# Re-laying copies behind units' products, and weight sums in earlier stretches, in a fused attention and feed-forward kernel

## The chip, the cores and the metric

The kernel runs on one core of a Trainium2 chip. The metric is the device time of one execution in microseconds. A core has a matrix engine (TensorE, PE in the profile), a vector engine (VectorE, DVE), an engine for activation functions (ScalarE, ACT), GpSimd (POOL), and a queue engine (SyncE, SP) that issues transfers. Each engine takes its instructions in the order in which they were written for it, and waits at an instruction until what it needs is there. Inputs and weights are in device memory; SBUF and PSUM are the core's own memories. [...]

## The reference

```python
B, H, S, D = 8, 12, 448, 64              # batches, heads, tokens, head size
scores = q @ k.transpose(0, 1, 3, 2) / sqrt(D) - log(S)
attn = 1 / (1 + exp(-scores))            # a sigmoid, no softmax
x = (attn @ v)                           # heads side by side: 3584 tokens x 768
gate = maximum(x @ w_gate, 0)            # 768 x 1536
val = x @ w_val                          # 768 x 1536
out = (gate * val) @ w_out               # 1536 x 768, float32
```

## The kernel before, in words

**Staging.** The kernel is software-pipelined over the eight batches: while TensorE does the attention of batch b it also does the feed-forward part of an earlier batch, in pieces put between pieces of attention. The order on every engine is written out by hand.

**Attention.** A batch has three groups of four heads (g) and seven chunks of 64 keys (c), so 21 score units. One unit (`qk_unit`, its products in line 239) makes scores into two PSUM banks, and ScalarE applies the sigmoid (line 187). When a group's seven chunks are there, `pv_group` multiplies with v (line 257) into two banks, and VectorE copies the result to the transposed activations xT (line 184).

**Feed-forward.** One unit (`gv`, lines 322 to 343) makes a gate and a value product (`g_ps`, `v_ps`, one bank each) for 128 of the 1536 inner columns; the gate goes through a relu on ScalarE (line 334) or VectorE (line 336), and VectorE multiplies it with the value into hT (line 343). When that product is done, the unit's value bank can be used again. Banks are given out in turn from a ring of eight (`bank`). A score unit, a PV group and a feed-forward unit each take two.

**Batch 1** has six stretches. Each is a burst of 3, 3, 3, 4, 4 or 4 score units, and then `ffn_mix` with 4, 3, 3, 3, 3 or 4 feed-forward units of batch 0. The bursts of the fourth and the sixth stretch hold a PV group after their second score unit. Batch 2's first burst (four score units with a PV group after the second) comes right behind the sixth stretch. In the code stretches and bursts count from 0: the fifth stretch is `hooks[4]` and `given[4]`.

**Hooks.** `ffn_mix` counts `left`, the units still to do, down from the number of units to 0. At each count it first runs the hooks whose number is at least `left`, then as many steps of the weight sums as `given` says for that place, then one unit. So `(3, ...)` in a stretch of three units runs ahead of the first, `(2, ...)` behind the first, and `(0, ...)` behind the last.

**Re-laying batch 2.** From batch 2 on, the heads' q and k are transposed by a DMA. `dma_transposes(b, g)` lets VectorE copy the group's k and then its q into one buffer `rel` (line 222, two copies), and has SP issue one transposing DMA from it to `qkT` (line 226). There are two `rel` buffers, so group 2's copies of a batch need group 0's transposing DMA to have read. The copies of batch 2 also need its k and q loads, which POOL issued earlier, and its first burst needs `qkT` of group 0.

**Late loads.** `late_loads` re-lays batch 2's third group, lets POOL copy two numbers out of `qkT` of the second group (`hold`, line 863, so that POOL goes on only when that transposing DMA has landed), and then lets POOL issue the loads of batch 2's v, of batch 3's k and q, and of `wo`, the output weights.

**Weight sums.** The feed-forward part of batch 1 saves products by using sums of weight blocks. For four pairs of 128 inner columns VectorE makes them beforehand in batch 1: `early_sum_steps` gives four steps for a pair, one in place on `wv` (`gate_sums`, line 391) and then S2, S1 and S4 (lines 391, 584, 391), 128 x 768 each. That is 16 steps in a fixed order; `given` says how many of them run at each place of a stretch. The step in place on `wv` must come behind batch 0's units on those columns.

Of the kernel before, what the change touches and what calls it, by code (L numbers as in the profile page):

```python
# [18 lines left out]
def kernel(  # L19
# [87 lines left out]
    def load(b, g0, g1, which, c0=0, c1=NCH):  # L107
        for nm, t16, src in zip("kq", tiles_of(b), (k, q)):
            if nm in which:
                xs, cs = slice(2 * g0, 2 * g1), slice(c0 * D, c1 * D)  # L110
                nc.gpsimd.dma_start(t16[:, xs, cs], rows_of(src, b)[:, xs, cs])  # L111

    def load_v(b):
        v16 = tiles_of(b)[2]
        nc.gpsimd.dma_start(v16[:, 0::2, :], rows_of(v, b)[:, 0::2, :])
        for r in range(2):
            nc.gpsimd.dma_start(
                v16[64 - 64 * r : P - 64 * r, 1::2, :], rows_of(v, b)[64 * r : 64 * r + 64, 1::2, :]
            )
# [70 lines left out]
    def qkT_of(b, g):  # L190
        if (b, g) not in qkT_tiles:
            qkT_tiles[(b, g)] = qkTp.tile([P, TW, P], FP16, tag="qkT", name="qkT")
        return qkT_tiles[(b, g)]
# [24 lines left out]
    def dma_transposes(b, g):  # L218
        k16, q16, _ = in_tiles[b]
        rel = relp.tile([P, TW, P], FP16, tag="rel", name="rel")  # L220
        for ti, t16 in enumerate((k16, q16)):
            nc.vector.tensor_copy(  # L222
                rel[:, ti * NCH : (ti + 1) * NCH, :].rearrange("p c (h d) -> p h c d", h=2),
                t16[:, 2 * g : 2 * g + 2, :].rearrange("p h (c d) -> p h c d", c=NCH),
            )
        nc.sync.dma_start_transpose(
            qkT_of(b, g)[:], rel[:].rearrange("p c x -> p (c x)")
        )
# [70 lines left out]
    def qk_unit(b, g, c):  # L299
        ps = [bank("qk_ps") for _ in range(2)]  # L300
        qk(qkT_tiles[(b, g)], c, 0, NCH, lambda hh: ps[hh][:, 0:S])
        PT = PTp.tile([P, 2, S], FP16, tag="PT", name="PT")
        for hh in range(2):
            sigmoid(PT[:, hh, 0:S], ps[hh][:, 0:S])
        PT_tiles[(b, g, c)] = PT

    def pv_group(b, g):
        pv(b, g, 0, S, [PT_tiles.pop((b, g, c))[:, :, 0:S] for c in range(NCH)])
# [74 lines left out]
    def open_late():  # L383
        first_sbuf.close()
        pool = ctx.enter_context(tc.tile_pool(name="late", bufs=1))
        late["T"] = pool.tile([P, 4, HF, HM], FP16, tag="T", name="T")
        late["X"] = pool.tile([P, 3, HD, S], FP16, tag="X", name="X")
        late["sums"] = ctx.enter_context(tc.tile_pool(name="sums", bufs=2))
# [174 lines left out]
    def early_sum_steps(j, f):  # L563
        views = []
        for i in range(3 * j, 3 * j + 3):
            t = early.tile([P, 2, 512], FP16, tag=f"PT{i}", name="S")
            flat = t[:].rearrange("p a y -> p (a y)")[:, 0 : HD * 2 * P]
            views.append(flat.rearrange("p (x y) -> p x y", y=2 * P))
        yield lambda: gate_sums(f, f + 2)
        yield from unit_sum_steps(("s", f), f, views)  # L570
# [285 lines left out]
    def pv_finish(b):  # L856
        pv_group(b, NG - 1)
# [7 lines left out]
    def both(b, g):  # L865
        pe_transposes(b, g, 0)
        pe_transposes(b, g, 1)
# [15 lines left out]
    def push_group(g):  # L883
        tail = [("y", g, p) for p in range(3)]
        if g == 0:
            work.extend([("u", 1, 8), ("s", 1, 0), ("u", 1, 9), ("s", 1, 4), ("u", 1, 10), ("u", 1, 11)])
            work.extend([tail[0], ("t", g, 0), ("t", g, 1), *tail[1:]])
            return
        if g != 2:
            tail.insert(0, ("y", g, NPP) if g == 3 else ("t", g, 2))  # L890
        work.extend([("w", g, f) for f in range(0, NFC, 2)] + tail)
# [40 lines left out]
    for b in range(1, B):  # L932
        if b == 1:
            cuts, pv_at = (0, 3, 6, 9, 13, 17, 21), {3: (0, 2), 5: (1, 2)}
        else:
            cuts, pv_at = (0, 4, 7, 11, 14, 18, 21), {0: (-1, 2), 2: (0, 2), 4: (1, 2)}
        bursts = list(range(len(cuts) - 1))
        inner = {}
        if b > 2:
            inner = {0: 1, 3: 5} if b == 3 else {0: 1} if b % 2 == 0 else {2: 3, 3: 5} if b == B - 1 else {4: 5}  # L940
            for n in inner.values():
                bursts.remove(n)
        count = len(bursts)
        hooks = {}
        if b == 1:
            mix = (4, 3, 3, 3, 3, 4)
            hooks = {
                1: [(3, lambda: both(1, 1))],
                3: [(3, lambda: both(1, 2))],
                4: [(3, lambda: dma_transposes(2, 0)), (1, lambda: dma_transposes(2, 1))],  # L950
                5: [(4, late_loads)],
            }
            steps = itertools.chain.from_iterable(early_sum_steps(j, 2 * j) for j in range(4))
            given = ((0, 0, 1, 1, 1), (0, 1, 1, 0), (0, 1, 1, 1), (0, 1, 1, 0), (2, 0, 0, 0), (0, 1, 1, 1, 1))
        else:
            mix = (0,) * count

        def burst(n):
            for i, (g, c) in enumerate(order[cuts[n] : cuts[n + 1]]):
                if n in pv_at and i == pv_at[n][1]:  # L960
                    if n == 0:
                        pv_finish(b - 1)
                        if b == 2:
                            push_group(0)
                        elif b % 2 == 0:
                            push_group(b // 2 - 1)
                    else:
                        pv_group(b, pv_at[n][0])
                qk_unit(b, g, c)

        for m in range(count):
            jobs, ahead = [], []
            burst(bursts[m])
            if m == 0 and b > 3:
                jobs.append(lambda: dma_transposes(b, 2))
            if b == 2 and m == 2:
                ahead.append(lambda: dma_transposes(3, 0))
            elif b == 2 and m == 3:
                jobs.append(lambda: dma_transposes(3, 1))
            elif b == 3 and m == count - 1:  # L980
                jobs.append(lambda: dma_transposes(4, 1))
            elif 0 <= m - count + 2 and 3 < b < B - 1:
                jobs.append(lambda: dma_transposes(b + 1, m - count + 2))
            if b == 1:
                if m == 0:
                    load(2, 0, 1, "kq")
                    load(2, 1, 2, "kq")
                    load(2, 2, 3, "kq")
            elif m == 0 and b + 1 < B:
                for g0, g1 in ((0, 1), (1, NG)) if b == 3 else ((0, NG),) if b > 3 else ():  # L990
                    jobs.append(lambda g0=g0, g1=g1: load(b + 1, g0, g1, "kq"))
                jobs.append(lambda: load_v(b + 1))
            if b == 2 and m == 0:
                ahead.append(lambda: split_sums(1))
            elif b == 2 and m == 4:
                open_late()
                first_sums = token_sum_steps(0, 0)
                ahead += [*first_sums[:2], lambda: weight_sums(0)]
            elif b == 2 and m == 5:
                ahead += [lambda: weight_sums(1), lambda: dma_transposes(3, 2)]  # L1000
                jobs += first_sums[2:]
            elif b == 3 and m == 0:
                jobs.append(lambda: (weight_sums(2), weight_sums(3)))
            elif b == 3 and m < 3:
                jobs.append(lambda: gate_sums(6 + 2 * m, 8 + 2 * m))
            if b % 2 and b > 2:
                if m == count - 1:
                    jobs.append(lambda: (batch_sums_t1(b // 2), batch_sums(b // 2, (0, 1))))
            elif b > 3 and m == 0:
                jobs.append(lambda: batch_sums(b // 2 - 1, (1, HD)))  # L1010
            if mix[m]:
                for job in jobs:
                    job()
                ffn_mix(mix[m], hooks.get(m, ()), steps, given[m])
            else:
                next_work(
                    jobs, ahead=ahead,
                    amid=(lambda: burst(inner[m])) if m in inner else None,
                )
            if b == 3 and m == count - 2:  # L1020
                dma_transposes(4, 0)
# [35 lines left out]
```

## Time and profile before

| what | value |
|---|---|
| three runs | 389.72 us median (389.47 to 389.98) |
| profiled execution, its own time | 390.76 us |
| its span, first to last instruction | 388.9 us |
| mean granted clock of TensorE | 0.998 |
| TensorE busy | 382.5 us, 98% of the span |
| VectorE busy | 300.1 us, 77% |
| ScalarE busy | 227.6 us, 59% |
| GpSimd busy | 49.9 us, 13% |
| instructions | 8973 |

A row of a timeline reads: start in us from the span's start, duration in us, engine, line of the kernel, operation, output<-input, shape, and in brackets the idle time of the engine before it and what ended it. Instructions of one kind that follow each other are merged (x12). Of the merged ones the duration reaches from the first start to the last end, and ends overlap the next start. A row of the chain that ended last reads: start, duration, what. A row of stretches of time reads: from:to, the time in it, then busy time and number of instructions of PE, PEld (weight load), DVE, ACT and POOL, then the granted clock, the mean busy share of the DMA engines, and GB/s.

### The profile page before, as it was taken

The numbers are of one execution on the slowest core, as the hardware profiler recorded it, in microseconds if no ns is written. First come the engines' busy times: TensorE is split into PE (matmuls) and PEld (weight loads), VectorE is DVE, ScalarE is ACT, GpSimd is POOL, SyncE is SP. The second block draws the span as 40 slices with busy tenths as digits, with TensorE's granted clock in tenths as the row PEclk, the third lists the DMA queues.
The fourth block names the chain that finished last, engine by engine and source line by source line (L and its number), as shares of the span: only waits on it lengthen the run. The fifth ranks groups of instructions, "written<-read, shape, count | busy, mean of one in ns | idle before, by whom it ended". The sixth has DMA issues, their size and how long they took to land.

```text
span 388.9 us, 8973 instructions
## 1 busy us (share of the span) xinstructions
PE 382.5 (98%) x3576; PEld 224.3 (58%) x3576; DVE 300.1 (77%) x595; ACT 227.6 (59%) x480; POOL 49.9 (13%) x73
## 2 busy tenths in 40 slices
PE   8999999999999999999999999999999999999995
PEld 5678776975555545454455554545455555555663
DVE  2455667769767799999757789999987788999553
ACT  5967777577797755555547764545477344333321
POOL 7643406100400300003000300000000000000000
PEclk9999999999999999999999999999999999999999
DMA  9999999999997990226945794222012220000336
GB/s 171 198 199 204 204 171 167 207 196 154 166 200 150 150 230 12 48 49 86 174 88 131 129 228 69 40 57 49 1 32 69 74 74 1 2 0 2 81 82 164
DMA packets 68987, 43.81 MB, mean 113 GB/s; under 512 B 35664, under 2 KB 65616, under 8 KB 68944
## 3 DMA queue, kind: packets, MB, share of 16 engines
q0 software_dynamic: 30496, 23.24, 39.6%
q1 hardware_dynamic: 37664, 19.24, 24.4%
q10 hardware_dynamic: 784, 0.75, 0.6%
q8 instruction: 28, 0.46, 0.5%
q14 instruction: 15, 0.12, 0.1%
HBM read 47.19 MB, written 11.01 MB: 150 GB/s over the span
## 4 chain that ended last, share of the span: by engine, by line
PE 89%; DMA 7%; DVE 1%; issue 1%; POOL 1%; ACT 0%; DVEq 0%; POOLq 0%; ACTq 0%
PE u L400 34%; PE g L400 16%; PE y L400 11%; PE qk_ps L239 8%; PE pv_ps L257 7%; PE g_ps L322 3%; PE v_ps L322 3%; DMA q<-in_q_dram 3%; PE u L714 2%; DMA wv<-in_moe_w_val_dram 2%; DMA k<-in_k_dram 2%; PE g L714 2%; PE ya L366 1%; PE yb L366 1%; PE trt L204 0%
## 5 line engine op out<-in xcount | busy, mean ns | idle before, releaser
L187 ACT ACTIVATE PT<-qk_ps 128x448 f16<-128x448 f32 (+3 forms) x318 | 151.3, 584 | 81.4 <-PE qk_ps L239 81.0
L400 PEld LDWEIGHTS <-S 128*128 128x128 f16 x558 | 54.6, 98 | 44.7
L633 DVE TENSOR_TENSOR gsb<-g,gsb 128x448 f32<-128x448 f32 x72 | 42.9, 624 | 10.1 <-PE g L400 9.5
L239 PE MATMUL qk_ps<-qkT 64*64 64x448 f16 (+2 forms) x756 | 47.6, 336 | 0.3
L400 PEld LDWEIGHTS <-hT 128*128 128x128 f16 x306 | 28.5, 98 | 22.7 <-issue 5.2
L629 ACT COPY gsb<-u 128x448 f32<-128x448 f32 x48 | 25.6, 557 | 24.0 <-PE u L400 22.9
L257 PE MATMUL pv_ps<-PT,v 64*64 64x448 f16 (+2 forms) x756 | 37.2, 329 | 0.1
L184 DVE TENSOR_SCALAR xT<-pv_ps 128x448 f16<-128x448 f32 (+2 forms) x53 | 27.8, 566 | 9.6 <-PE pv_ps L257 8.2
L458 ACT ACTIVATE ysb<-u 128x384 f32<-128x384 f32 x30 | 14.7, 491 | 33.9 <-PE u L400 29.4
L400 PEld LDWEIGHTS <-wg 128*128 128x128 f16 x216 | 20.2, 98 | 21.8 <-issue 4.3
L400 PEld LDWEIGHTS <-wv 128*128 128x128 f16 x216 | 21.1, 98 | 19.7
L476 DVE SCALAR_TENSOR_TENSOR ysb<-y,ysb 128x384 f32<-128x384 f32 x29 | 16.1, 556 | 17.9 <-PE y L400 10.8
L239 PEld LDWEIGHTS <-qkT 64*64 64x64 f16 x756 | 17.9, 105 | 20.5 <-issue 14.5
L111 POOL DMA_DIRECT2D k<-in_k_dram x14 | 10.8, 775 | 142.6 <-DVE rel L222 136.8
L257 PEld LDWEIGHTS <-v 64*64 64x64 f16 x756 | 22.0, 107 | 11.1 <-issue 1.4
L400 PE MATMUL u<-T,hT 128*128 128x384 f16 x132 | 25.1, 327 | 0.0
L400 PE MATMUL u<-xT,wg 128*128 128x448 f16 x108 | 23.5, 354 | 0.0
L400 PE MATMUL u<-xT,wv 128*128 128x448 f16 x108 | 23.4, 352 | 0.0
L400 PE MATMUL g<-X,S 128*128 128x448 f16 x108 | 23.4, 352 | 0.0
L400 PE MATMUL g<-xT,S 128*128 128x448 f16 x108 | 23.4, 352 | 0.0
L400 PE MATMUL u<-X,wv 128*128 128x448 f16 x108 | 23.4, 352 | 0.0
L400 PE MATMUL g<-xT,wg 128*128 128x448 f16 x108 | 23.4, 352 | 0.0
(94 smaller groups left out, 563.5 us busy)
## 6 DMA issues: line engine op xcount, KB each, us to landing
out_dram<-ysb SPq DMA_DIRECT2D x52, 192.0 KB, 2.9
v<-in_v_dram POOLq DMA_DIRECT2D x8, 336.0 KB, 14.3
v<-in_v_dram POOLq DMA_DIRECT2D x16, 168.0 KB, 14.2
k<-in_k_dram POOLq DMA_DIRECT2D x4, 672.0 KB, 11.3
q<-in_q_dram POOLq DMA_DIRECT2D x4, 672.0 KB, 14.3
k<-in_k_dram POOLq DMA_DIRECT2D x9, 224.0 KB, 12.3
q<-in_q_dram POOLq DMA_DIRECT2D x7, 224.0 KB, 12.4
wo<-in_moe_w_out_dram POOLq DMA_DIRECT2D x1, 1536.0 KB, 19.2
```

What stands on the lines that cost most here:

```text
L111: nc.gpsimd.dma_start(t16[:, xs, cs], rows_of(src, b)[:, xs, cs])
L184: nc.vector.tensor_scalar(out=xT, in0=src, scalar1=XSCALE, scalar2=None, op0=AOP.mult)
L187: nc.scalar.activation(PT_ap, ps_ap, AF.Sigmoid, bias=sig_bias, scale=qk_scale)
L239: nc.tensor.matmul(out_of(hh)[o : o + 64, :], qkT[rows, c, cols], qkT[rows, NCH + c0 : NCH + c1, cols], start=True, stop=True, tile_positi ...
L257: nc.tensor.matmul(ps[hh][64 * r : 64 * r + 64, 0:qn], v16[rows, 2 * g + hh, c * D : (c + 1) * D], pieces[c][rows, hh, :], start=(c == 0), ...
L322: nc.tensor.matmul(ps[:, 0:qn], (wg, wv)[i][:, dc, f * P : (f + 1) * P], xT_tiles[b][:, dc, q0 : q0 + qn], start=(dc == 0), stop=(dc == ND ...
L400: nc.tensor.matmul(ps[:, 0:n], A[:, k_, :], W[:, k_, :], start=(first and k_ == 0), stop=(k_ == kn - 1), skip_group_check=True,)
L458: nc.scalar.activation(o, ps[:, 0:HM], AF.Copy, scale=OUT_SCALE)
L476: nc.vector.scalar_tensor_tensor(out=o, in0=ps[:, 0:HM], scalar=OUT_SCALE, in1=o, op0=AOP.mult, op1=AOP.add)
L629: by(gs[u][i][:], ps[u][:, 0:S])
L633: nc.vector.tensor_tensor(out=gs[u][i][:], in0=ps[u][:, 0:S], in1=gs[u][i][:], op=AOP.add)
L714: nc.tensor.matmul(ps[j // 2][:, j % 2 * SQ : (j % 2 + 1) * SQ], sets[j][i][:, k_, :], W[:, k_, :], start=(first and j % 2 == 0 and k_ == ...
```

## The change

Hooks and numbers of steps in batch 1 are changed; no operation is added or taken away.

```diff
                 1: [(3, lambda: both(1, 1))],
                 3: [(3, lambda: both(1, 2))],
-                4: [(3, lambda: dma_transposes(2, 0)), (1, lambda: dma_transposes(2, 1))],
-                5: [(4, late_loads)],
+                4: [(2, lambda: dma_transposes(2, 0)), (0, lambda: dma_transposes(2, 1))],
+                5: [(2, late_loads)],
             }
             steps = itertools.chain.from_iterable(early_sum_steps(j, 2 * j) for j in range(4))
-            given = ((0, 0, 1, 1, 1), (0, 1, 1, 0), (0, 1, 1, 1), (0, 1, 1, 0), (2, 0, 0, 0), (0, 1, 1, 1, 1))
+            given = ((0, 0, 1, 1, 1), (0, 1, 1, 1), (0, 2, 1, 1), (0, 1, 1, 0), (2, 0, 0, 0), (0, 1, 1, 0, 0))
```

In the fifth stretch, batch 2's first group is re-laid behind the first unit, not ahead of it, and the second group behind the third unit, not ahead of it. In the sixth, `late_loads`, with the third group's copies in it, comes behind the second of four units, not ahead of the first. The second stretch does three steps of the sums (two before), the third four (three before; two of them behind its first unit), the sixth two (four before); the first, fourth and fifth do three, two and two as before. Since the steps keep their order, each stretch from the second to the sixth does steps that a later place did before. The two steps at the head of the fifth stretch were the last pair's S1 and S4 of columns 512 to 767 before; now they are the step in place on `wv` and S2 of columns 768 to 1023.

## The prediction

> **What bounds the kernel now.** I read the share of busy time first, then the chain that ended last in order of time, then TensorE and VectorE instruction by instruction around the fifth stretch, then the third, and last what the DMA engines moved there. All times are from the one profiled execution: its span is 388.9 us, its own time 390.76 us, so 1.86 us lie around the span. The median of the runs shown is 389.72 us, 1.04 us less. I form a difference on the profiled execution and take it off the median. About 0.2% (0.78 us) is what a measurement of this kernel can tell from no change.
>
> ```profile
> PE 382.5 (98%) x3576; PEld 224.3 (58%) x3576; DVE 300.1 (77%) x595; ACT 227.6 (59%) x480; POOL 49.9 (13%) x73
> ```
>
> TensorE is busy in 98% of the span, so only its few holes can be won. They don't show as idle time: a matmul that waits for its PSUM bank is drawn long. The chain shows where one is.
>
> ```profile
> 40.46 12.42 DMA q<-in_q_dram
> 52.90 0.39 DVE rel L222
> ...
> 55.46 0.36 DVE hT L343
> 55.87 1.51 PE pv_ps L257 x26
> ```
>
> Up to 52.88 us the chain is a transfer: batch 2's first query tile, 12.42 us from issue to landing. Then VectorE, then a product of TensorE that waited. From there to the end of the span the chain is TensorE all but unbroken, so what is won or lost between 43 and 62 us stays in the total.
>
> VectorE in the fifth stretch (start, duration, instruction, and in brackets the idle time before it):
>
> ```profile
> 51.79 0.39 DVE L222 COPY rel<-k 128x896 f16<-128x896 f16 x1 [0.78 <-DMA k<-in_k_dram]
> 52.90 0.39 DVE L222 COPY rel<-q 128x896 f16<-128x896 f16 x1 [0.72 <-DMA q<-in_q_dram]
> 53.21 0.55 DVE L584 TENSOR_TENSOR S<-S,wg 128x768 f16<-128x768 f16 x1
> ...
> 54.15 0.42 DVE L336 TENSOR_SCALAR gate_sb<-g_ps 128x256 f32<-128x256 f32 x1
> 54.67 0.42 DVE L343 TENSOR_TENSOR hT<-gate_sb,v_ps 128x256 f16<-128x256 f32 x1
> ...
> 55.46 0.35 DVE L343 TENSOR_TENSOR hT<-gate_sb,v_ps 128x192 f16<-128x192 f32 x1
> ...
> 59.31 0.39 DVE L222 COPY rel<-k 128x896 f16<-128x896 f16 x1 [0.91 <-DMA qkT<-rel]
> ```
>
> The two copies idle VectorE 0.78 + 0.72 us for their inputs, and the outputs of the stretch's units (L336, L343), which empty their PSUM banks, queue behind them. The last line is a third wait, 0.91 us in the sixth stretch, for a buffer that a transposing DMA still reads.
>
> TensorE in the attention burst of the fourth stretch (first four lines) and of the sixth (last four); both are two score units, one PV group, two score units:
>
> ```profile
> 43.91 0.57 PE L239 MATMUL qk_ps<-qkT 64*64 64x448 f16 x8
> 44.31 1.49 PE L257 MATMUL pv_ps<-PT,v 64*64 64x448 f16 x28
> 45.63 0.55 PE L239 MATMUL qk_ps<-qkT 64*64 64x448 f16 x8
> 46.11 0.58 PE L204 MATMUL trt<-ident,k 128*64 128x128 f16 x14
> ...
> 54.81 0.71 PE L239 MATMUL qk_ps<-qkT 64*64 64x448 f16 x8
> 55.41 1.97 PE L257 MATMUL pv_ps<-PT,v 64*64 64x448 f16 x28
> 57.03 0.72 PE L239 MATMUL qk_ps<-qkT 64*64 64x448 f16 x8
> 57.69 0.83 PE L322 MATMUL g_ps<-xT,wg 128*128 128x256 f16 x6
> ```
>
> From first line to next work the fourth stretch's burst takes 46.11 - 43.91 = 2.20 us, the sixth's 57.69 - 54.81 = 2.88. The same burst at the head of batch 2 (62.39 to 64.60) takes 2.21. So the hole is 2.88 - 2.21 = 0.67 us. The eight banks go round in pairs: a pair taken by a unit's two products is asked for again four pairs later. So the second score unit needs the first unit's hT product done, the PV group the second's, the third score unit the third's. The trace bears it out: second hT done at 55.82, PV goes on at 55.87.
>
> **The change part by part.** No instruction is added or removed; order changes on VectorE, and with it when SP and POOL get their work.
>
> Copies of batch 2's first group, from ahead of the fifth stretch's units to behind the first one. The waits for k (landed 51.8) and q (52.88) go, because VectorE reaches them later. Working with TensorE 0.29 us late (next part): the two sums now at the head of the stretch run 51.2 to 52.2 (0.47 apart, as in the third stretch). The first gate product ends at 52.54, L336 runs at 52.65, the value product ends at 53.19, hT 53.30 to 53.72; copies 53.63 and 53.93 (0.30 apart, as at 55.73 and 56.03); L336 of the second unit 54.24, its hT 0.45 later (55.01 to 55.46 before) 54.69 to 55.04; third hT 55.28 to 55.63. TensorE asks for these at about 55.3, 55.48 and 56.8. All three are in time, so the whole 0.67 us goes. Ends: nothing gained, if the inputs of the timed runs land early enough that there was no hole, and 0.67 as seen. I take 0.67, the row itself.
>
> Sums, earlier. The second stretch's extra one (0.55 us) falls into the 2.63 us that VectorE idles before 42.91: nothing; without that cover it would hold the third stretch's first hT by 0.47. The third stretch gets two sums, not one, between its first and second unit:
>
> ```profile
> 42.91 0.35 DVE L343 TENSOR_TENSOR hT<-gate_sb,v_ps 128x192 f16<-128x192 f32 x1 [2.63 <-ACT gate_sb L334]
> 43.18 0.55 DVE L391 TENSOR_TENSOR S<-wv 128x768 f16<-128x768 f16 x1
> 43.65 0.41 DVE L343 TENSOR_TENSOR hT<-gate_sb,v_ps 128x256 f16<-128x256 f32 x1
> ```
>
> The second hT moves from 43.65 to 44.12 and ends at 44.53. The PV group at 44.31 uses its bank, and by the sixth stretch's rhythm (goes on at 55.87, next work at 57.69, so 1.82 us before the burst's end) it asks at 46.11 - 1.82 = 44.29. So TensorE waits until 44.58: 0.29 us, new. The third hT ends at 45.33, asked for near 45.9: no cost. Ends of this term: 0 and 0.47 (the whole sum). I take 0.29. The fourth stretch keeps two sums beside its units, which keep their 0.2 to 0.5 us of VectorE idle time; the sixth has two fewer.
>
> Second group's copies, from ahead of the third unit to behind it: they run at 55.5 and 55.8 before the xT copies, which wait for the PV group until 57 anyway: nothing.
>
> Late loads and the third group's copies, from ahead of the sixth stretch's units to behind the second. TensorE's units there ran without a hole (57.69 to 62.39), so the 0.91 us wait gives nothing. What follows on the queues: SP's first transpose is issued at about 54.32 and not 53.38, the second at 56.3 (56.49 before, SP's first issue lasting 2.23 us), the third at 61.2 (60.08). POOL's marker copy waits for the second one's landing: 56.3 + 4.3 = 60.6 against 60.8, so the loads behind it (v of batch 2, k and q of batch 3, wo) are issued where they were. If the first transpose holds up the second by its whole delay, they are 0.9 us late.
>
> Sum: -0.67 + 0.29 = -0.38 us; 390.76 becomes 390.38, the median 389.72 becomes 389.34, 389.3 us (-0.10%).
>
> [...] POOL's DMA issues at 43.06 and 44.16 took 0.72 us each beside a VectorE without a gap: no block shows. [...]
>
> The first transpose was issued at 53.38 and landed 5.8 us later, while the last load of batch 2 landed at 57.36; the engines moved this (the last number of a line is GB/s):
>
> ```profile
> 56.50:57.00 0.50, 0.50 (x17) 0.37 (x13) 0.18 (x1) 0.50 (x2) 0.00 (x0) 1.00 0.18 16
> ...
> 57.50:58.00 0.50, 0.50 (x9) 0.29 (x4) 0.50 (x2) 0.40 (x1) 0.00 (x0) 1.00 1.27 290
> ```
>
> [...]
>
> **The rivals.**
> Slower: the first transposed tile lands late. VectorE now meets the third group's copies at 60.5, in the middle of four units, and they need the first transpose's buffer. Behind them are 0.6 us of copies, 0.47 of a sum and the third hT (0.35), asked for by batch 2's first PV group at about 62.35. So a landing after 60.8, 6.5 us after issue, decides, and each further microsecond is one of TensorE. Against it: 5.8, 4.3 and 4.0 us for these three transposes. For it: 14.5 and 14.1 us for batch 3's first two at 79.6 and 83.8 beside loads. At 8 us the price is 1.5: -0.38 + 1.5, 390.8 us.
>
> Faster: the input tiles land later in the timed runs. The changed order takes q until 53.93 at no cost, 1.05 us later than seen; the old one lost every microsecond of it. The six loads took 12.4 to 13.2 us, so 0.4 to 0.8 us later is possible: gain 1.07 to 1.47 less 0.29, 388.9 to 388.5 us.
>
> No hole in the timed runs: their inputs land a microsecond earlier (they are 1.04 us shorter as a whole), nothing is won, the 0.29 is lost: 390.0 us.
>
> [...]
>
> **How the numbers follow.** Forecast 0.33; no hole 0.10 and late wo 0.05, which also end within 0.2%: 0.48 together. Faster by over 0.2%: 0.27, the later landing. Slower by over 0.2%: 0.25, the late transpose with 0.20 and 0.05 for it with other loads held up behind it. The range runs from the faster rival's 388.6 to 390.9 just above the slower one at 8 us; the forecast's own is 389.0 to 390.0.
>
> **What would show it.** Right: no wait for k or q in VectorE's fifth stretch; sixth burst 2.2 us; fourth burst 2.5 us; qkT of the first group landed by 60.8; batch 2's first burst 2.2 us. Wrong: a long PV matmul at 62, a wait of VectorE for the transposing DMA above 0.3 us, or T<-wo with idle time near 93 us.

## The result, and the profile after

Twelve executions of the changed kernel took 394.99 us in the median, against 389.72 us for twelve of the kernel before; the ratio is 1.0108 with a 95% interval from 1.0076 to 1.0141, so the change made the kernel slower by about 1.1%. (The ratio compares means and leaves out the two longest executions of the changed kernel, so it is smaller than that of the medians.) The forecast was 389.3 us, and the time is outside its range. The changed kernel's executions spread far more than those before: two took 389.71 and 390.68 us, the other ten 393.74 to 397.27, while the kernel before stayed between 389.24 and 390.00. The profile that came with the result is of the 390.68 us execution, as long in span as the one before (388.9 us both). A long one was profiled in the first experiment. Both are shown, since the short one shows what the change did where it was meant to act, and the long one where the time went.

TensorE in the short execution, in the bursts of the fourth and the sixth stretch:

```profile
43.01 0.57 PE L239 MATMUL qk_ps<-qkT 64*64 64x448 f16 x8
43.41 1.78 PE L257 MATMUL pv_ps<-PT,v 64*64 64x448 f16 x28
44.84 0.72 PE L239 MATMUL qk_ps<-qkT 64*64 64x448 f16 x8
45.50 0.58 PE L204 MATMUL trt<-ident,k 128*64 128x128 f16 x14
...
54.20 0.57 PE L239 MATMUL qk_ps<-qkT 64*64 64x448 f16 x8
54.60 1.49 PE L257 MATMUL pv_ps<-PT,v 64*64 64x448 f16 x28
55.92 0.55 PE L239 MATMUL qk_ps<-qkT 64*64 64x448 f16 x8
56.41 0.83 PE L322 MATMUL g_ps<-xT,wg 128*128 128x256 f16 x6
```

The sixth burst takes 56.41 - 54.20 = 2.21 us: no hole. The fourth takes 45.50 - 43.01 = 2.49, before 2.20: the new wait of 0.29 us is there to the hundredth. VectorE no longer waits for the copies' inputs (start, duration, no idle time in brackets):

```profile
52.66 0.39 DVE L222 COPY rel<-k 128x896 f16<-128x896 f16 x1
52.97 0.38 DVE L222 COPY rel<-q 128x896 f16<-128x896 f16 x1
...
93.71 1.36 DVE L391 TENSOR_TENSOR T<-wo 128x2304 f16<-128x2304 f16 x1 [1.60 <-DMA wo<-in_moe_w_out_dram]
```

The last line is what is new: at 93.71 us, in batch 2's fifth stretch, VectorE waited 1.60 us for the output weights wo. Before, they had landed when it got there (no idle time in brackets), and the hT product behind the sum was done at 95.19 us, 0.48 us ahead of the value product that needs the bank it empties:

```profile
93.31 1.35 DVE L391 TENSOR_TENSOR T<-wo 128x2304 f16<-128x2304 f16 x1
94.58 0.61 DVE L343 TENSOR_TENSOR hT<-gate_sb,v_ps 128x448 f16<-128x448 f32 x1
95.67 1.30 PE L322 MATMUL v_ps<-xT,wv 128*128 128x448 f16 x6
```

In the short execution TensorE lost 1.10 us to the wait and was back at the times of the kernel before (its first product with wo starts at 99.08 us, before at 99.11).

The long execution (395.95 us, span 394.2), the chain that ended last:

```profile
66.27 31.08 DMA wo<-in_moe_w_out_dram
97.34 0.02 issue
97.37 0.04 DVE T L391
97.40 1.24 issue
98.64 0.62 DVE hT L343
99.27 0.04 issue
99.31 2.18 PE v_ps L322 x6
101.49 0.89 PE qk_ps L239 x8
102.38 1.69 PE pv_ps L257 x28
```

The second half of wo took 31.08 us from issue to landing, before 26.4. Behind it stand VectorE's first sum of wo, the hT product queued behind that, and TensorE's value product, which waits for the bank that hT empties. The waits and TensorE of the same execution (waits: engine, line, what it waited for, total, times, longest):

```profile
DVE T L391 <- DMA wo<-in_moe_w_out_dram: 3.7, 1, 3.7
PE v_ps L322 <- DVE hT L343: 3.2, 1, 3.2
```

```profile
94.83 1.31 PE L322 MATMUL g_ps<-xT,wg 128*128 128x448 f16 x6
99.31 2.18 PE L322 MATMUL v_ps<-xT,wv 128*128 128x448 f16 x6 [3.17 <-DVE hT L343]
101.42 0.96 PE L239 MATMUL qk_ps<-qkT 64*64 64x448 f16 x8
102.17 1.90 PE L257 MATMUL pv_ps<-PT,v 64*64 64x448 f16 x28
```

After a stand of 3.17 us TensorE is slow as well: the value product takes 2.18 us, against 1.29 us in the short execution. The stretches of time show why (the third number from the end is the granted clock):

```profile
96.00:98.00 2.00, 0.13 (x1) 0.00 (x0) 0.63 (x1) 1.72 (x4) 0.00 (x0) 1.00 1.25 194
...
100.00:101.00 1.00, 1.00 (x4) 0.30 (x2) 1.00 (x3) 0.00 (x0) 0.00 (x0) 0.50 1.22 124
101.00:102.00 1.00, 1.00 (x10) 0.37 (x12) 0.54 (x2) 0.00 (x0) 0.76 (x2) 0.50 0.67 73
```

The clock was 1.00 while TensorE stood, and 0.50 from 99.6 to 103.0 us. From the value product to the first product with wo it took 104.38 - 99.31 = 5.07 us; in the short execution 99.08 - 95.65 = 3.43. So 1.6 us are lost to the clock, on top of the 3.2 of the stand: 4.8 us, close to the 5.3 between the medians.

### The profile page after: what moved, and what is told of

It is laid out like the page before. It is cut to its first block, busy times and chain, and to the rows that moved or that the text cites. A ratio compares the mean times of both kernels' runs of the same rounds, so it can differ in the third digit from the quotient of the medians.

```text
span 388.9 us, 8974 instructions
## 1 busy us (share of the span) xinstructions
PE 382.0 (98%) x3576; PEld 224.3 (58%) x3576; DVE 299.8 (77%) x595; ACT 227.4 (58%) x480; POOL 49.9 (13%) x73
## 4 chain that ended last, share of the span: by engine, by line
PE 73%; DMA 16%; issue 5%; POOL 3%; DVE 1%; ACT 0%; POOLq 0%; DVEq 0%; ACTq 0%
PE u L400 34%; PE g L400 16%; PE y L400 11%; DMA wo<-in_moe_w_out_dram 7%; PE qk_ps L239 6%; PE pv_ps L257 5%; DMA k<-in_k_dram 3%; DMA q<-in_q_dram 3%; DMA wg<-in_moe_w_gate_dram 2%; POOL q L111 1%; PE ya L366 1%; PE yb L366 1%; POOL k L111 1%; POOL v L115 0%; ACT PT L187 0%
## 5 line engine op out<-in xcount | busy, mean ns | idle before, releaser
L322 PE MATMUL v_ps<-xT,wv 128*128 128x256 f16 (+2 forms) x168 | 22.8, 273 | 1.1 <-DVE hT L343 1.1
L400 PE MATMUL u<-X,S 128*128 128x448 f16 x108 | 23.4, 352 | 0.0
```

Source lines behind the costliest of these rows:

```text
L322: nc.tensor.matmul(ps[:, 0:qn], (wg, wv)[i][:, dc, f * P : (f + 1) * P], xT_tiles[b][:, dc, q0 : q0 + qn], start=(dc == 0), stop=(dc == ND ...
L400: nc.tensor.matmul(ps[:, 0:n], A[:, k_, :], W[:, k_, :], start=(first and k_ == 0), stop=(k_ == kn - 1), skip_group_check=True,)
```

## The experiments

Each is compared with the kernel before on the same chip. Twelve kernels were run.

**Which part, and which wait.** First the change once more:

> The changed kernel once more, for a profile of one of its long executions: of twelve, ten took 393.7 to 397.3 us and two 389.7 and 390.7, and the one profiled so far took 390.7. In that one the second half of wo landed at 93.7 us instead of 92.4, VectorE waited 1.60 us for it and TensorE 1.10 us. Theory A (late weights): the third transposing DMA, now issued together with POOL's late loads, holds these up; in a long execution wo lands some 5 us later still, and VectorE's wait before T<-wo is 5 us or more. Theory B (late transposed tile): in a long execution the first transposed tile of batch 2 lands after 60.8 us and TensorE stands at 61 us for some 5 us, while the wait for wo is 2 us or less. About 395 us by both.

Measured: 394.83 us (389.69 to 396.48), ratio 1.0095 (1.0058 to 1.0132). Its profile is the long execution shown above. The first transposed tile landed 4.4 us after issue and batch 2's first burst had no hole, so theory B falls. Theory A holds, with a size off: wo landed 3.7 us later than in the short execution and 5.0 us later than before, and VectorE, which reached the place 1.6 us later than in the short one, waited 3.7 us, not 5.

These are the two transfers that theory A names, in the kernel before (first two rows) and in the long execution (last three). v is the first of the late loads, SPq is SP's queue, and a row without a start ends with the time from issue to landing:

```profile
qkT<-rel SPq DMA_TRANSPOSE x1, 4.0
61.28 0.76 POOL L115 DMA_DIRECT2D v<-in_v_dram  x1 [0.30 <-PE g_ps L322]
...
61.59 0.76 POOL L115 DMA_DIRECT2D v<-in_v_dram  x1 [0.20 <-PE v_ps L322]
61.73 3.51 SPq L226 DMA_TRANSPOSE qkT<-rel  x1
qkT<-rel SPq DMA_TRANSPOSE x1, 13.5
```

Before, the third transposing DMA was issued at 60.08 us, 1.2 us ahead of v, and landed 4.0 us later. In the long execution it was issued 0.1 us behind v and took 13.5 us. The next runs put the late loads back, and then change one part at a time.

```diff
-                5: [(2, late_loads)],
+                5: [(4, late_loads)],
```

> The changed kernel with the late loads, the third group's copies among them, put back ahead of the sixth stretch's units; copies of the fifth stretch and weight sums stay as changed. Theory A: the third transposing DMA has moved its data before the loads start, wo lands by 92.5 us, and what is left is the hole that closes, less the new wait in the fourth stretch: 389.0 to 389.7 us, and none above 391. Theory B: the first transpose is still issued behind the first unit, so it stays at about 395 us.

Measured: 389.67 us (389.45 to 390.24), ratio 1.0006 (0.9997 to 1.0015). With the late loads back in place, the loss is gone.

The kernel before with `5: [(2, late_loads)]` alone:

> The kernel before with only the late loads put behind the second unit of the sixth stretch. Theory A: this part alone makes the loss, 393 to 396 us in most executions. Theory B: the first transpose is issued where it was, so 389.5 to 390 us.

Measured: 394.24 us (393.78 to 394.99), ratio 1.0120 (1.0105 to 1.0135). This part alone makes the whole loss. Its profile shows the same wait at wo:

```profile
94.93 1.36 DVE L391 TENSOR_TENSOR T<-wo 128x2304 f16<-128x2304 f16 x1 [2.77 <-DMA wo<-in_moe_w_out_dram]
```

POOL issued the loads no later than before: the marker was read at 59.41 us here, when TensorE was 1.24 us ahead of the kernel before (its sixth burst ended its units at 61.15, before at 62.39), so at about the same place of the program as the 60.80 before. What is late is the third transposing DMA, issued at 60.48 behind the loads' first issue at 59.89; before it was issued at 60.08, ahead of 61.28. It took 12.7 us to land, not 4.0.

The kernel before with the changed `given` alone:

> The kernel before with only the numbers of weight sums changed as in the change. Both theories: no transfer is moved, so within 0.3 us of the kernel before: plus 0.29 us if the extra wait of the fourth stretch stays in the total, nothing if the chain there still runs through the landing of q. Were the sums the cause of the loss, it would be near 395 us.

Measured: 389.93 us (389.39 to 390.38), ratio 1.0009 (1.0000 to 1.0018), so +0.4 us where +0.29 stood in the forecast.

**What the third transposing DMA does to the loads.** The changed kernel with the marker on the third tile:

```diff
-        hold(2, 1)
+        hold(2, 2)
```

> The changed kernel with POOL's marker copy waiting for the third transposed tile and not for the second, so that the late loads are issued only when the third transposing DMA has landed: some 3.6 us later than before (60.3 + 4.0 + 0.5 = 64.9 against 61.28 us). Theory A, that the third transposing DMA and the loads hurt each other when in flight together: the loads are issued later and wo lands earlier than in the long executions, by 94.5 us; TensorE waits under 1.5 us, its clock stays, 389.7 to 391.3 us. Rival C, that only the moment of issue counts (wo late because POOL gets to it late, or VectorE's work holds POOL up): wo lands at 96 us or later, 393 to 396 us.

Measured: 394.12 us (393.01 to 395.28), ratio 1.0120 (1.0097 to 1.0142). Theory A missed. The marker came at 66.09 us, not 64.4, because the third DMA was issued at 61.11 and took 4.9 us. The loads themselves were quicker than before (k 7.8 us, not 9.6; the second half of wo 25.0, not 26.4), but they were issued 5.3 us later than before, and wo landed at 96.3. So lateness needs no meeting of the two.

```profile
66.09 0.32 POOL L863 COPY gate<-qkT 1x2 f16<-1x2 f16 x1 [22.21 <-DMA qkT<-rel]
```

The third group transposed by TensorE, as batch 1's are:

```diff
     def late_loads():
-        dma_transposes(2, 2)
+        both(2, 2)
```

> The changed kernel with batch 2's third group transposed by TensorE, as batch 1's groups are, at the same place, so there is no third transposing DMA and the loads go as in the change. It costs TensorE some 0.9 us (46.11 to 47.02 for batch 1's third group). Theory A: wo lands by 92.5 us in every execution, no wait before T<-wo, 390.2 to 391.0 us. Rival C: the loads are issued at the same moment as in the change, so wo stays late: 393 to 396 us.

Measured: 390.96 us (390.55 to 392.02), ratio 1.0045 (1.0029 to 1.0061). With the loads issued when the change issues them (60.77 us), but no third transposing DMA, wo landed at 89.9 and nobody waited for it. Rival C falls.

The kernel before with `hold(2, 0)`, the loads earlier:

> The kernel before with the marker copy waiting for the first transposed tile and not for the second, so that the late loads are issued some 1.5 us earlier, while the third transposing DMA (issued at 60.1) and perhaps the second are in flight. Theory A: the same loss without any part of the change, 393 to 396 us in most executions, the third tile landing 9 us or more after issue. Rival C: loads issued earlier land earlier, 389.5 us.

Measured: 389.91 us (389.36 to 390.46), ratio 1.0010 (1.0001 to 1.0019). Theory A missed again: the two did run together, the third tile took 11.2 us, and the engines' rate fell as in the bad kernels (the last number is GB/s):

```profile
67.00:68.00 1.00, 1.00 (x18) 0.64 (x11) 0.73 (x2) 0.74 (x2) 0.24 (x1) 1.00 2.43 178
68.00:69.00 1.00, 1.00 (x13) 1.00 (x11) 0.74 (x2) 1.00 (x4) 0.00 (x0) 1.00 0.68 23
```

But the loads had started 2.4 us earlier, and wo landed at 92.8.

The kernel before with the fifth stretch's hooks alone (`4: [(2, ...), (0, ...)]`):

> The kernel before with only the fifth stretch's copies behind the first and the third unit; the weight sums and the late loads as before. No new wait in the fourth stretch, since the sums stay. If the hole of 0.67 us in the sixth burst is in the timed executions of the kernel before too: 388.9 to 389.1 us. If it is there only where the query tile lands late, as the profiles of the last two experiments suggest (their sixth bursts take 2.2 us with the copies in their old places): 389.4 to 389.7 us, no measurable change.

Measured: 389.61 us (389.31 to 390.13), ratio 1.0005 (0.9997 to 1.0014). No gain: the hole of 0.67 us is not a part of the usual execution. In the profiles of the third and the fourth experiment the copies stood in their old places and the sixth burst took 2.21 us too; q was waited for 0.69 us in one and not at all in the other.

**The theory after eight runs.** Neither the meeting nor the moment of issue alone decides, but both eat the same thing, the time in which the DMA engines move the loads. From 74 to 80 us all of these kernels move 206 to 208 GB/s, so what counts is what was moved before:

| kernel | third transpose issued, us | v issued, us | GB/s 60 to 74 us | wo landed, us | VectorE waits, us | median, us |
|---|---|---|---|---|---|---|
| before | 60.1 | 61.3 | 171 | 92.4 | 0 | 389.7 |
| changed, short | 60.4 | 60.6 | 148 | 93.7 | 1.6 | (390.7) |
| changed, long | 61.7 | 61.6 | 108 | 97.4 | 3.7 | 394.8 |
| late loads ahead | 59.2 | 60.9 | 180 | 91.4 | 0 | 389.7 |
| only late loads behind | 60.5 | 59.9 | 138 | 94.9 | 2.8 | 394.2 |
| sums only | 59.3 | 60.4 | 179 | 92.4 | 0.4 | 389.9 |
| marker after third | 61.1 | 66.6 | 108 | 96.3 | 3.1 | 394.1 |
| third by TensorE | none | 60.8 | 159 | 89.9 | 0 | 391.0 |
| marker after first | 59.2 | 58.8 | 169 | 92.8 | 0 | 389.9 |
| fifth stretch only | 59.1 | 60.7 | 183 | 92.2 | 0 | 389.6 |

Each row is of one profiled execution, and the median is of all of the kernel's; the value in brackets is that one execution's own time. wo's landing is its issue from POOL's rows plus its time to landing. The rate counts the transposing DMA's own bytes too, 128 x 1792 values of 2 bytes or 459 KB: with the third group on TensorE these were not to be moved, and 159 GB/s were enough.

From v's issue to wo's landing the table gives 29.1 us without a third transposing DMA and 29.7 where it had landed before v was issued, 30.5 to 32.0 where it was issued 1.2 us or more ahead of v, and 33.1 to 35.8 where it was issued within 0.6 us of v. In that time the DMA engines moved 5.2 MB in the first two cases and 5.6 to 6.0 MB in all others, so what differs among the others is the mean rate: 188 GB/s before, 163 in the long execution. In the changed kernel, whose loads were issued about when they were before, the meeting is therefore what costs. With the marker after the first tile it cost as well (34.0 us, before 31.1), and there the 2.4 us of earlier issue made up for it.

For the long execution and the kernel before the rows from 60 to 74 us read:

```profile
60.00:74.00 14.00, 14.00 (x163) 11.08 (x161) 9.53 (x21) 9.42 (x22) 8.00 (x11) 1.00 1.06 108
```

```profile
60.00:74.00 14.00, 14.00 (x163) 11.09 (x161) 10.04 (x21) 9.41 (x22) 7.90 (x11) 1.00 1.08 171
```

At 207 GB/s the missing 63 x 14 = 882 KB are 4.3 us, and wo landed 97.4 - 92.4 = 5.0 us later. Some of that was idle time, some slow transfer. One row of the long execution shows each, where the mean busy share of the DMA engines stands ahead of the rate:

```profile
62.00:63.00 1.00, 1.00 (x19) 0.63 (x20) 0.73 (x3) 0.50 (x2) 1.00 (x3) 1.00 0.00 0
...
68.00:69.00 1.00, 1.00 (x13) 1.00 (x11) 0.54 (x1) 1.00 (x4) 0.58 (x2) 1.00 1.58 71
```

Between 61 and 63 us the engines move nothing (0 GB/s), as v was issued at 61.6 and the third transposing DMA at 61.7; near 68 us they are marked busy and move a third of their rate (71 GB/s, against 206 from 74 to 80 us), with the transposing DMA and the loads in flight together.

Two runs put that to the test. The changed kernel with `hold(2, 0)`:

> The changed kernel with the marker copy waiting for the first transposed tile, so that the late loads are issued some 1.5 to 2 us earlier and the third transposing DMA stays where the change puts it. After the last four runs neither being in flight together alone (it was, at +0.1%) nor the moment of issue alone explains the loss. Theory D (a DMA budget): wo lands when the loads have had their DMA time; between 60 and 74 us the engines moved 171 GB/s in the kernel before, 183 and 180 in the good variants, 148, 138, 108 and 108 in the bad ones, whether lost by idling or by slow transfers, and wo followed. Loads issued 1.5 to 2 us earlier fill the idle part, so the mean from 60 to 74 us comes to 150 GB/s or more, wo lands by 94 us and most of the loss goes: 389.7 to 391.5 us. Theory A as first put (together means late): still 393 to 396 us.

Measured: 390.79 us (389.94 to 392.40), ratio 1.0037 (1.0019 to 1.0054). Of the 5 us, 4 are gone, though the third transposing DMA is as late as in the change and took 13.8 us. The mean rate is 163 GB/s, wo landed at 92.8, and VectorE waited 0.20 us:

```profile
92.84 1.36 DVE L391 TENSOR_TENSOR T<-wo 128x2304 f16<-128x2304 f16 x1 [0.20 <-DMA wo<-in_moe_w_out_dram]
```

The changed kernel with `5: [(3, late_loads)]`:

> The changed kernel with the late loads behind the first unit of the sixth stretch, not the second: the third transposing DMA is issued some 0.8 us earlier than changed and some 0.5 us later than with the late loads ahead of the units, so between. Theory D: the third tile is issued 0.6 to 1.0 us ahead of v (before 1.2, changed -0.1 to 0.2), most of its data is moved before the loads': 389.6 to 391 us, wo by 93.5 us. If any delay of the third transpose tips it over: 393 to 396 us.

Measured: 389.88 us (389.40 to 390.88), ratio 1.0008 (0.9998 to 1.0017). The third tile was issued at 59.63 us, 0.7 ahead of v, and took 7.1 us; 176 GB/s, wo at 92.1, no wait. Both came out as the DMA budget had it. Both profiles are of the shortest execution of their kernel (389.94 and 389.40 us), so in the median one wo may land later than they show.

**What the stand costs.** The kernel before with VectorE kept busy for a known time ahead of the same hT product, no transfer moved:

```diff
-                ahead += [*first_sums[:2], lambda: weight_sums(0)]
+                ahead += [*first_sums[:2], *[lambda: weight_sums(0)] * 2]
```

> The kernel before with the first sum of wo (T<-wo, 1.27 us of VectorE) made twice at its place, no transfer changed: VectorE is late there by a known time. It has 0.48 us before the next value product needs its bank, so TensorE should stand for about 0.8 us. If only the standing costs: +0.8 us, 390.3 us. If a stand of this length also lowers the granted clock: 391.5 us or more. In the profile of the changed kernel's short execution a stand of 1.10 us left the clock at 1.00, so 390.3 us is expected.

Measured: 390.60 us (390.18 to 392.13), ratio 1.0028 (1.0014 to 1.0041). That is 1.0 us more than before (389.56 us). In the profile, which is of the shortest execution, TensorE stood 0.81 us, as worked out, and its clock stayed at 1.00.

With `* 4` in place of `* 2`:

> The kernel before with the first sum of wo made four times: VectorE late by 3.81 us, TensorE standing for about 3.3 us, as in the long executions of the changed kernel (3.17 us), with no transfer changed. If what follows there belongs to the stand (granted clock 0.50 for some 3.3 us, 1.6 us lost): 3.3 + 1.6, 394.4 us, with the clock at 0.50 behind it. If it belongs to the transfers: +3.3, 392.8 us, clock at 1.00.

Measured: 395.34 us (394.68 to 395.64), ratio 1.0141 (1.0120 to 1.0162). A stand of 3.59 us cost 5.8 us:

```profile
97.87 2.40 PE L322 MATMUL v_ps<-xT,wv 128*128 128x448 f16 x6 [3.59 <-DVE hT L343]
```

```profile
97.00:98.00 1.00, 0.13 (x1) 0.10 (x1) 1.00 (x3) 0.00 (x0) 0.00 (x0) 0.50 0.03 8
...
102.00:103.00 1.00, 1.00 (x16) 0.54 (x12) 0.00 (x0) 0.68 (x2) 0.75 (x2) 0.50 1.05 165
```

So the half clock belongs to the stand and not to the transfers, and it cost more than the expected 1.6 us: from the value product to the first product with wo 103.95 - 97.87 = 6.08 us, not 3.43.

## Why the prediction was wrong, point by point

- **What bounds the kernel.** Right for TensorE, but incomplete: from 60 us to 92 us the DMA engines were a second bound with almost no room. wo landed at 92.4 and was read at 93.31. The page's row for DMA showed nines there. (A wait can also show as idle time, which the prediction says it doesn't: the stand of 3.17 us does, ahead of the value product.)
- **Copies of the first group, -0.67 us.** The profile of the change looks as forecast (no wait, burst 2.21 us), but the burst is as short in the third and fourth experiments, with the copies in their old places, so this doesn't show the mechanism at work. As a gain it failed: the hole was in the one profiled execution, 1.04 us longer than the median, and isn't in the usual ones (389.61 against 389.46 us with this part alone). This was the rival "no hole in the timed runs", which had 0.10. Its reason, earlier inputs, isn't shown: in the third experiment VectorE waited 0.69 us for q, and there was no hole.
- **The faster rival**, with 0.27, needed the hole to be larger in the timed runs. It was not there, so nothing of it came.
- **Sums earlier, +0.29 us.** Right: 0.29 us in the trace. Alone it measured +0.4 us (0.0 to 0.7), which agrees but hardly tells it from nothing. The second stretch's extra sum cost nothing. (In the text on the change, the two steps at the head of the fifth stretch before are the third pair's, not the last pair's.)
- **Late loads behind the second unit, "the loads behind it (...) are issued where they were".** This is the step that failed. The sentence itself is about true: the first load was issued at 60.62 us in the short execution and 61.59 in the long one, 61.28 before. But the third transposing DMA, which the same paragraph moves from 60.08 to 61.2 us, was given no price and no reason for having none: the paragraph doesn't ask what that transfer does to the loads. It left the DMA engines idle first and then shared them with the loads, and the second half of wo landed 1.3 and 5.0 us later than before. Its own lateness (9.3 and 13.5 us to landing) hurt nobody, as TensorE first reads its tile at about 89 us; the loads beside it did.
- **The slower rival.** The wrong transfer: the first transposed tile landed after 4.8 and 4.4 us. The row it was priced by (14.5 us beside loads) was the right row, for the third tile. The 0.05 for "other loads held up behind it" names the effect that came, with the wrong transpose and without a price.
- **Late wo.** T<-wo with idle time near 93 us, the last sign of being wrong that the prediction names, is what came. VectorE's 3.67 us of waiting less the 0.48 us of room gives 3.19, and TensorE stood 3.17; in the short execution 1.60 less 0.48 gives 1.12, and it stood 1.10. The prediction's chance of 0.05 for late wo, with an end within 0.2% of no change, rests on no run: the second half of wo landed 1.3 us (short execution) and 5.0 us (long one) later than before, and behind a stand of 3.17 us came 1.6 us of half clock, which the prediction doesn't price.
- **POOL's issues, "no block shows".** POOL's issues of the late loads took 0.76, 1.25, 0.86, 0.84 and 2.04 us in the changed kernel, before 0.76, 1.26, 0.87, 0.84 and 2.04, so nothing held them. But this is no test of a block by the copies: in the profile of the change these were over at 60.35 us, and the first issue came at 60.62, beside other operations of VectorE.

Not settled: why the transposing DMA and the loads together move so little, and what lets two of twelve executions of the changed kernel escape, and two of ten in the first experiment. The short and the long profile differ in where the third issue falls against v's (0.2 us ahead, 0.1 behind), but that is one execution of each. No variant beat the kernel before.

## What to carry to other kernels

When a transfer moves, follow not only who reads its result but which transfers are behind it in the same DMA engines and how much room those have; a second bound doesn't show in the chain of waits until it takes over (the load of wo is not in the chain before, and 31.08 us of it in the long execution). A hole seen in one profiled execution that is longer than the median is a candidate, not yet a gain. And where TensorE is the bound, price a stand as long as those here (2.3 us and more) by its length plus the slow stretch that follows.

## What the runs showed of the hardware

The granted clock fell to 0.50 after stands of TensorE of 2.27 us (only the late loads behind), 2.64 (marker after the third tile), 3.17 (the long execution) and 3.59 us (sum made four times). It did not after 0.81 us (one more sum) and 1.10 us (the short execution). It fell 0.3 to 1.0 us after work had begun again in three cases, and within the stand, after some 2.3 us, in the longest. It stayed down for 3.4 us in the first three cases and for 6.8 in the last.

The busy share of the DMA engines says little about what they move: 1.58 went with 71 GB/s (the long execution, 68 to 69 us, loads and a transposing DMA) and 1.25 with 207 (the short one, 74 to 80 us).
